# GpSimd takes the softmax divisions and six copies of means in the lead; the last token tile is finished in halves

## Chip, cores and metric
One Trainium2 chip; the kernel runs on one of its cores. The metric is the device time of one execution in microseconds (us). Engines: TensorE (PE, its weight loads PEld), VectorE (DVE), ScalarE (ACT), GpSimd (POOL), SyncE (SP, which issues the DMAs).

## What is computed
Local attention for 2 batches, 8 heads, 768 positions and heads of 64, then two feed-forward layers over the 1536 tokens (model width 512, hidden width 2048), all in float32:

```python
k_sum = k.reshape(B, H, nb, 32, D).max(axis=3)
v_sum = v.reshape(B, H, nb, 32, D).mean(axis=3)
scores_l = scale * q @ k.T where |i - j| < 16 else -1e9
scores_s = scale * q @ k_sum.T + log(32)
a = softmax(concat([scores_l, scores_s]))
x = a @ concat([v, v_sum])                    # (1536, 512)
x = maximum(x @ w_in, 0) ** 2 @ w_out         # first layer
h = x @ w_in2;  out = (h * sigmoid(h)) @ w_out2
```

## The kernel before
Attention works on 24 tiles of 64 queries (12 a batch). A tile's 8 heads lie as 4 pairs; each query sees 96 window keys and 24 block keys, 120 columns (NK). For a tile g: scores `pss` (TensorE, 16 products), minus the scores with the mask and the row minimum (VectorE, `minimum`, line 414, from PSUM with the mask in SBUF), exponentials with their sums z (ScalarE, line 419), a guard and the reciprocal r (VectorE, lines 439 and 442), the division T*r (`norm`, lines 445 to 450), transposes `psa` (TensorE, line 456), their copy a (ScalarE), products `av` with the values (TensorE), and then x split into a high part (ScalarE) and a low part (VectorE).

The layers use three float32r products for one exact one: high by high, high by low, low by high. Every weight arrives as raw 64-bit numbers and is decoded: a scale `c` on ScalarE, a shift (line 306), a sign (310) and a join (314) on VectorE, then a high part on ScalarE and a low part on VectorE (262). Blocks of 512 tokens go through 16 chunks of the hidden width: h (`gemm1`), relu and square, split, `gemm2` into four accumulators.

The **lead** is tiles 0 to 7 (NLEAD), the 512 tokens of the first block. Until all eight have their x, no h can run. Their value tiles are one tile `vlead`: 96 rows by DMA, 24 rows with the block means, the same for all tiles of the batch. The means come out of six products `psv`, and ScalarE copies them from PSUM into eight tiles (`vmean`, two instructions of four tiles each).

The order of the whole first part (the lead, the first layer's first two blocks, the other 16 attention tiles) on every engine and on SP's queue is written by `first_order`: a list scheduler with a cost and a due time for each step, the due times moved by a table `shift`; the kernel then issues the steps in that order. Later blocks are plain loops. `layer2_block` is the second layer: chunk by chunk, with `rows` giving each token tile of 128 its products; the last two chunks (LAG) are taken tile by tile, each tile is then copied out of PSUM, VectorE and ScalarE in turn, and stored by SP.

## Time and profile before

| | us |
|---|---|
| runs | 610.33 median of 3 (609.83 to 612.03) |
| profiled execution | 611.61 |
| its span | 609.6 |
| TensorE busy | 595.1 |
| VectorE busy | 326.4 |
| ScalarE busy | 323.4 |
| GpSimd busy | 9.6 |

The span is from the first to the last instruction that the profiler saw; the execution's own time has 2.0 us more around it. Busy times are sums over the whole span, so they hide that stretches differ. TensorE's mean granted clock was 0.997 of full.

### The profile page before, as it was taken

Reading aid. Unit: us, or ns where it says so; the run is one execution under the profiler, and the core shown is the slowest. Engines: PE = TensorE matmul, PEld = TensorE weight load, DVE = VectorE, ACT = ScalarE, POOL = GpSimd, SP = SyncE. Lnnn points to the kernel's source line nnn. Section 1 sums busy time; section 2 is a strip of 40 time slices with the busy share of each in tenths; the row PEclk is TensorE's granted clock in tenths of the full one; section 3 lists DMA queues with packets and bytes.
Section 4 is the critical chain, followed back from the end, with each engine's and each line's share of the span. In section 5 each row is a group of like instructions: output and inputs, shape, how many; then the busy total and the mean of one; then the engine's idle time right before and its main releaser. Section 6 shows DMA issues by size and latency. Waiting matters only on the chain.

```text
span 609.6 us, 8844 instructions
## 1 busy us (share of the span) xinstructions
PE 595.1 (98%) x3242; PEld 483.3 (79%) x3242; DVE 326.4 (54%) x779; ACT 323.4 (53%) x727; POOL 9.6 (2%) x25
## 2 busy tenths in 40 slices
PE   6999999899999999999999999999999999999997
PEld 5578788668987878888888888888888888888886
DVE  4999999994433332385556686764322222322222
ACT  4999987788766764565555554443321222212221
POOL 0000000110000000000000000000000000000000
PEclk8999999999999999999999999999999999999999
DMA  8987888676545642365662345425400223400211
GB/s 301 300 281 271 291 294 271 229 253 223 182 170 164 215 152 94 115 203 184 199 202 74 105 138 184 161 104 187 158 0 2 91 84 103 138 1 5 99 35 69
DMA packets 36618, 96.50 MB, mean 158 GB/s; under 512 B 3936, under 2 KB 11232, under 8 KB 36576
## 3 DMA queue, kind: packets, MB, share of 16 engines
q1 hardware_dynamic: 36576, 95.95, 47.8%
q8 instruction: 25, 0.41, 0.3%
q14 instruction: 17, 0.14, 0.1%
HBM read 74.96 MB, written 20.97 MB: 157 GB/s over the span
## 4 chain that ended last, share of the span: by engine, by line
PE 78%; DVE 6%; DMA 3%; ACT 1%; issue 0%; SPq 0%; ACTq 0%
PE acc L254 38%; PE h L254 37%; DMA t_kv<-in_vT_dram 2%; PE pss L254 2%; PE av L254 1%; PE psa L456 1%; DMA raw_wi<-in_w_in_dram 1%; DMA kw<-in_kW_dram 1%; DVE raw_wi L310 1%; DVE c_wo L314 1%; DVE c_wi L314 1%; DVE vsumT L637 1%; DVE g L262 0%; DVE raw_wo L310 0%; DVE wi L262 0%; DVE wo L262 0%
## 5 line engine op out<-in xcount | busy, mean ns | idle before, releaser
L254 PE MATMUL h<-xt,wi 128*128 128x512 f32 (+1 forms) x600 | 141.9, 385 | 0.5 <-DVE xt L262 0.4
L254 PE MATMUL acc<-g,wo 128*128 128x512 f32 (+1 forms) x600 | 141.5, 384 | 0.0
L254 PE MATMUL h<-xt,wj 128*128 128x512 f32 x576 | 139.0, 390 | 0.0
L254 PEld LDWEIGHTS h<-xt,wj 128*128 128x128 f32 x576 | 108.1, 188 | 23.6 <-DVE r L262 0.2
L254 PEld LDWEIGHTS h<-xt,wi 128*128 128x128 f32 x600 | 108.3, 188 | 22.9 <-DVE xt L262 0.7
L254 PEld LDWEIGHTS acc<-g,wo 128*128 128x128 f32 x600 | 108.2, 188 | 22.3 <-issue 1.0
L262 DVE TENSOR_TENSOR g<-r,g 128x512 fp32r<-128x512 f32 (+1 forms) x98 | 67.1, 685 | 70.5 <-ACT g L258 69.9
L262 DVE TENSOR_TENSOR r<-h,r 128x512 f32<-128x512 f32 x48 | 33.2, 692 | 114.3 <-ACT r L510 113.7
L510 ACT ACTIVATE r<-h 128x512 f32<-128x512 f32 x48 | 28.7, 598 | 117.4 <-PE h L254 117.4
L258 ACT ACTIVATE g<-r 128x512 fp32r<-128x512 f32 (+1 forms) x98 | 61.0, 623 | 35.8 <-DVE r L262 34.5
L254 PE MATMUL acc<-wq,g 128*128 128x512 f32 x240 | 57.3, 389 | 0.0
L254 PE MATMUL acc<-wo,g 128*128 128x512 f32 x216 | 53.6, 397 | 0.0
L254 PEld LDWEIGHTS acc<-wq,g 128*128 128x128 f32 x240 | 45.1, 188 | 9.3
L254 PEld LDWEIGHTS acc<-wo,g 128*128 128x128 f32 x216 | 40.6, 188 | 9.7
L419 ACT ACTIVATE T<-T,m 128x120 f32<-128x120 f32 x96 | 36.6, 384 | 6.1 <-DVE m L414 6.1
L693 ACT ACTIVATE r<-h 128x512 f32<-128x512 f32 (+1 forms) x34 | 19.1, 561 | 24.3 <-PE h L254 24.3
L254 PE MATMUL acc<-wp,g 128*128 128x512 f32 x120 | 28.8, 389 | 0.0
L506 ACT ACTIVATE r<-h 128x512 f32<-128x512 f32 x16 | 9.6, 597 | 36.0 <-PE h L254 36.0
L254 PEld LDWEIGHTS acc<-wp,g 128*128 128x128 f32 x120 | 22.5, 188 | 4.7
L414 DVE CUSTOM_DVE_ANT_0 T<-pss,cst_sb 128x120 f32<-128x120 f32 x96 | 21.8, 274 | 5.3 <-PE pss L254 5.1
L262 DVE TENSOR_TENSOR wj<-c_wj,wj 128x512 fp32r<-128x512 f32 x16 | 11.1, 692 | 22.6 <-ACT wj L258 22.6
L448 ACT ACTIVATE T<-T,r 128x120 f32<-128x120 f32 x64 | 20.0, 383 | 2.4 <-DVE r L442 2.4
(78 smaller groups left out, 540.8 us busy)
## 6 DMA issues: line engine op xcount, KB each, us to landing
raw_wo<-in_w_out_dram SPq DMA_DIRECT2D x22, 512.0 KB, 4.4
wq<-split SPq DMA_DIRECT2D x20, 512.0 KB, 3.3
raw_wi<-in_w_in_dram SPq DMA_DIRECT2D x16, 512.0 KB, 5.0
split<-wo SPq DMA_DIRECT2D x16, 512.0 KB, 3.1
raw_wj<-in_w_in_dram SPq DMA_DIRECT2D x16, 512.0 KB, 4.0
wo<-split SPq DMA_DIRECT2D x16, 512.0 KB, 3.3
raw_wp<-in_w_out_dram SPq DMA_DIRECT2D x10, 512.0 KB, 3.6
split<-wp SPq DMA_DIRECT2D x10, 512.0 KB, 2.8
```

The lines of the kernel that those rows point to most:

```text
L254: pe.matmul(o, l, r, **kw)
L258: return act.activation(out=o, in_=i, func=AF.Copy, scale=scale)
L262: return eng.tensor_tensor(out=o, in0=a, in1=b, op=op)
L310: vec.scalar_tensor_tensor(out=low, in0=high, scalar=SIGN, in1=low, op0=ALU.bitwise_and, op1=ALU.bitwise_or)
L314: vec.scalar_tensor_tensor(out=c, in0=c, scalar=3, in1=raws.pop(name)[:, :, 0], op0=ALU.logical_shift_left, op1=ALU.bitwise_or)
L414: vec.tensor_tensor_reduce(out=d["T"][:, c], in0=d["ps"][:, c], in1=cst_sb[:, kind * NK:kind * NK + NK], scale=-0.125, scalar=3.0e38, op0= ...
L419: act.activation(out=d["T"][:, c], in_=d["T"][:, c], func=AF.Exp, bias=d["m"][:, c:c + 1], scale=-1.0, accum_out=d["z"][:, c:c + 1])
L448: act.activation(out=T[:, c], in_=T[:, c], func=AF.Copy, scale=r[:, c:c + 1])
L456: pe.transpose(ps[0:NK, c], d["T"][:, c], id_sb)
L506: act.activation(out=r, in_=h, func=AF.Relu)
L510: act.activation(out=r, in_=h, func=AF.Sigmoid)
L693: act.activation(out=rs[n][:, cc], in_=hs.pop(n)[:, cc], func=AF.Relu)
```

## The change
GpSimd takes two things over in the lead. It divides the exponentials by their sums for tiles 0 to 7 (VectorE did), and ScalarE copies the means from PSUM to tiles 0 and 1 alone; GpSimd copies them on from there, within SBUF, to tiles 2 and 3 and then to tiles 4 to 7. The planner's table, some due times and the distance of loads are changed, so the order of the whole first part is another one. In the second layer the very last token tile's last two chunks, copy and store are done in two halves of 256 columns.

```diff
+MEANS = [(2, 4), (4, 8)]
...
-    shift = dict(psl=-3,ttl=3,exl=-6,ze=-4,nt=2,psa=-6,a=-0.5,vs=1,vmean=1,av=0.5,xh=-2,xl=-2,ksl=0.5,kwl=3,ksum=-6)
+    shift = dict(psl=-2,ttl=2,nt=0.5,psa=-6,a=2,vs=3,ksl=2,kwl=-1,ksum=1)
...
-        return 0.25 * g if g < NLEAD else 50 + 14 * (g - NLEAD) if g < TPB else 120 + 4 * (g - TPB) if g < 2 * NLEAD else 155 + 10 * (g - 2 * NLEAD)
+        return 0.25 * g if g < NLEAD else 50 + 20 * (g - NLEAD) if g < TPB else 120 + 4 * (g - TPB) if g < 2 * NLEAD else 160 + 11 * (g - 2 * NLEAD)
...
-    for i in range(NLEAD // NGRP):
-        op("act", "vmean", i, 1.9, -5, [("vs", c, M) for c in range(6)] + [("vl", i, 0)] * 0)
+    op("act", "vmean", 0, 1.05, -5, [("vs", c, M) for c in range(6)])
+    for i, (g0, g1) in enumerate(MEANS):
+        op("pool", "vmore", i, .3 + .5 * (g1 - g0), -5 + i, [("vmean", 0, A)])
...
-            op("vec", "nt", g, .78, due, [("rc", g, .1)])
+            op("pool", "nt", g, 1.4, due, [("rc", g, A)])
...
-        load("raw", (x, s), 524, chunk_due(s) - 14 + .5 * (x == "wo") - 100 * (not i),
+        load("raw", (x, s), 524, chunk_due(s) - 18 + .5 * (x == "wo") - 100 * (not i),
...
-                load("c2", s, 262, due - 20, [("scr", s, 0), ("st2", chunks[i - NRAW], A) if s < NRAW else ("lo2", s - NRAW, A)])
+                load("c2", s, 262, due - 14, [("scr", s, 0), ("st2", chunks[i - NRAW], A) if s < NRAW else ("lo2", s - NRAW, A)])
...
-                vec.tensor_scalar(out=T[:, c], in0=T[:, c], scalar1=r[:, c:c + 1], scalar2=None, op0=ALU.mult)
+                eng.tensor_scalar(out=T[:, c], in0=T[:, c], scalar1=r[:, c:c + 1], scalar2=None, op0=ALU.mult)
...
+        def spread(eng, g0, g1, means):
+            copy(eng, vlead[NWIN:NK, g0:g1].rearrange("p g h d -> p g (h d)"),
+                 bass.AP(means.tensor, means.offset, [means.ap[0], [0, g1 - g0], [1, DM]]))
+
+        def vmean(_):
+            spread(act, 0, MEANS[0][0], psv[NWIN:NK])
+
+        def vmore(i):
+            spread(pool, *MEANS[i], vlead[NWIN:NK, 0])
...
+        parts = [(k, slice(0, DM)) for k in range(n // P)]
+        if tok0 + n == NTOK:
+            k = n // P - 1
+            parts[-1:] = [(k, slice(0, 256)), (k, slice(256, DM))]
         with tc.manual_schedule(engines={pe.engine}):
-            for k in range(n // P):
-                rows(acc[k], k, range(NF - LAG, NF), gs, wos)
-        for k in range(n // P):
-            o = raw_p.tile([P, 512], F32, tag="raw", name=f"ro{tok0}_{k}")
-            copy(act if k % 2 else vec, o, acc[k])
-            sp.dma_start(out=out[tok0 + k * P:tok0 + (k + 1) * P, :], in_=o)
+            for k, cols in parts:
+                rows(acc[k], k, range(NF - LAG, NF), gs, wos, cols)
+        for i, (k, cols) in enumerate(parts):
+            o = raw_p.tile([P, 512], F32, tag="raw", name=f"ro{tok0}_{i}")
+            copy(act if i % 2 else vec, o[:, cols], acc[k][:, cols])
+            sp.dma_start(out=out[tok0 + k * P:tok0 + (k + 1) * P, cols], in_=o[:, cols])
```

The order on GpSimd, from its last memset of the lead on (T is a tile's exponentials, r the reciprocals, qd a copy of queries for the later tiles 12 and up). Before:

```order
L569 MEMSET t_ksum0_2_178 128x16
L370 MEMSET share_108 32x1 x4
L569 MEMSET t_ksum0_3_180 128x16
L259 COPY qd0_101<-qr0_99 128x256
L259 COPY qd1_102<-qr1_100 128x256
```

Now, from the instruction behind that memset on (the ISA row sets GpSimd up for what follows):

```order
L452 ISA
L452 TENSOR_SCALAR T0_134<-T0_134,r0_138 128x120 x4
L452 TENSOR_SCALAR T1_139<-T1_139,r1_143 128x120 x4
L452 TENSOR_SCALAR T2_144<-T2_144,r2_148 128x120 x4
L452 TENSOR_SCALAR T3_149<-T3_149,r3_153 128x120 x4
L452 TENSOR_SCALAR T4_154<-T4_154,r4_158 128x120 x4
L452 TENSOR_SCALAR T5_159<-T5_159,r5_163 128x120 x4
L452 TENSOR_SCALAR T6_164<-T6_164,r6_168 128x120 x4
L452 TENSOR_SCALAR T7_169<-T7_169,r7_173 128x120 x4
L261 COPY vlead_105<-vlead_105 24x1024
L261 COPY vlead_105<-vlead_105 24x2048
L261 COPY qd0_101<-qr0_99 128x256
```

Eight tiles of four divisions and the two copies of means stand in front of the first copy of queries.

The order on ScalarE and VectorE before the first h. ScalarE first, from the exponentials of tile 6 before, and of tile 7 now (a is the copy of a tile's transposes, xt0 the high part of x, c and w the weights). Before:

```order
L419 ACTIVATE T6_164,z6_167<-T6_164,m6_166 128x120 x4
L419 ACTIVATE T7_169,z7_172<-T7_169,m7_171 128x120 x4
L258 ACTIVATE c_wi0_452<-raw_wi0_201 128x512
L258 ACTIVATE a3_150<-psa3_406 120x512
L258 ACTIVATE a4_155<-psa4_424 120x512
L258 ACTIVATE wi0_469<-c_wi0_452 128x512
L258 ACTIVATE vlead_105<-psv0_118 24x2048 x2
L258 ACTIVATE xt0_85<-av0_485 128x4x64
L258 ACTIVATE xt0_85<-av1_495 128x4x64
L258 ACTIVATE xt0_85<-av2_506 128x4x64
L258 ACTIVATE a5_160<-psa5_462 120x512
L258 ACTIVATE xt0_85<-av3_516 128x4x64
```

Now:

```order
L421 ACTIVATE T7_169,z7_172<-T7_169,m7_171 128x120 x4
L260 ACTIVATE a0_135<-psa0_349 120x512
L260 ACTIVATE a1_140<-psa1_371 120x512
L260 ACTIVATE c_wi0_447<-raw_wi0_201 128x512
L260 ACTIVATE vlead_105<-psv0_118 24x1024
L260 ACTIVATE a2_145<-psa2_442 120x512
L260 ACTIVATE wi0_473<-c_wi0_447 128x512
L260 ACTIVATE xt0_85<-av0_463 128x4x64
L260 ACTIVATE a3_150<-psa3_452 120x512
L260 ACTIVATE a4_155<-psa4_475 120x512
L260 ACTIVATE xt0_85<-av1_482 128x4x64
L260 ACTIVATE c_wo0_512<-raw_wo0_205 128x512
```

The copies of a of tiles 0 to 2, which stood among the exponentials, stand behind them, and the copies of means went from two of 24x2048 to one of 24x1024. VectorE's, from the first join of weights before and from the first shift now, before:

```order
L314 SCALAR_TENSOR_TENSOR c_wi0_452<-c_wi0_452,raw_wi0_201 128x512
L442 RECIPROCAL r7_173<-z7_172 128x4
L306 TENSOR_SCALAR raw_wo0_205<-raw_wo0_205 128x512
L450 TENSOR_SCALAR T7_169<-T7_169,r7_173 128x120 x4
L262 TENSOR_TENSOR wi0_469<-c_wi0_452,wi0_469 128x512
L310 SCALAR_TENSOR_TENSOR raw_wo0_205<-raw_wo0_205 128x512
L306 TENSOR_SCALAR raw_wi1_207<-raw_wi1_207 128x512
L310 SCALAR_TENSOR_TENSOR raw_wi1_207<-raw_wi1_207 128x512
L306 TENSOR_SCALAR raw_wo1_215<-raw_wo1_215 128x512
L310 SCALAR_TENSOR_TENSOR raw_wo1_215<-raw_wo1_215 128x512
L262 TENSOR_TENSOR xt0_85<-av0_485,xt0_85 128x4x64
L262 TENSOR_TENSOR xt0_85<-av1_495,xt0_85 128x4x64
```

Now:

```order
L308 TENSOR_SCALAR raw_wi0_201<-raw_wi0_201 128x512
L312 SCALAR_TENSOR_TENSOR raw_wi0_201<-raw_wi0_201 128x512
L316 SCALAR_TENSOR_TENSOR c_wi0_447<-c_wi0_447,raw_wi0_201 128x512
L308 TENSOR_SCALAR raw_wo0_205<-raw_wo0_205 128x512
L312 SCALAR_TENSOR_TENSOR raw_wo0_205<-raw_wo0_205 128x512
L264 TENSOR_TENSOR wi0_473<-c_wi0_447,wi0_473 128x512
L264 TENSOR_TENSOR xt0_85<-av0_463,xt0_85 128x4x64
L308 TENSOR_SCALAR raw_wi1_207<-raw_wi1_207 128x512
L312 SCALAR_TENSOR_TENSOR raw_wi1_207<-raw_wi1_207 128x512
L264 TENSOR_TENSOR xt0_85<-av1_482,xt0_85 128x4x64
L308 TENSOR_SCALAR raw_wo1_215<-raw_wo1_215 128x512
L264 TENSOR_TENSOR xt0_85<-av2_495,xt0_85 128x4x64
```

The divisions are gone, and the low parts of x stand one by one between the steps of the weights.

The order on TensorE around the first h (pss8 and pss9 are the scores of tiles 8 and 9, acc0 the first layer's accumulators). Before:

```order
L254 MATMUL av6_562<-a6_165,vlead_105 64x64 x8
L254 MATMUL av7_576<-a7_170,vlead_105 64x64 x8
L254 MATMUL pss9_587<-kw9_233,qr1_100 64x120 x8
L254 MATMUL h0_0_615<-xt0_85,wi0_469 128x512 x12
L254 MATMUL h0_1_645<-xt0_85,wi1_628 128x512 x12
L254 MATMUL pss8_680<-kw8_225,qr0_99 64x120 x8
L254 MATMUL acc0_0_694<-g0_0_666,wo0_603 128x512 x3
```

Now:

```order
L256 MATMUL av6_570<-a6_165,vlead_105 64x64 x8
L256 MATMUL av7_583<-a7_170,vlead_105 64x64 x8
L256 MATMUL h0_0_607<-xt0_85,wi0_473 128x512 x12
L256 MATMUL h0_1_637<-xt0_85,wi1_604 128x512 x12
L256 MATMUL pss8_667<-kw8_225,qr0_99 64x120 x8
L256 MATMUL acc0_0_681<-g0_0_658,wo0_543 128x512 x3
```

Tile 9's scores no longer stand ahead of h; they come after six more h and g products of the first layer.

## Rows read from the trace of the kernel before

**Rows 1.** The page, first part: busy us, share and instructions of each engine.
```profile
PE 595.1 (98%) x3242; PEld 483.3 (79%) x3242; DVE 326.4 (54%) x779; ACT 323.4 (53%) x727; POOL 9.6 (2%) x25
```

**Rows 2.** By stretch: length, busy of PE, PEld, DVE, ACT, POOL; clock, DMA, GB/s.
```profile
12.00:13.00 1.00, 1.00 (x12) 1.00 (x14) 0.97 (x3) 1.00 (x4) 0.00 (x0) 0.50 1.06 389
...
30.00:36.00 6.00, 4.59 (x128) 4.21 (x130) 5.64 (x16) 5.98 (x12) 0.00 (x0) 1.00 1.01 264
...
40.00:60.00 20.00, 20.00 (x102) 16.39 (x101) 19.72 (x53) 19.69 (x48) 0.00 (x0) 1.00 0.89 309
...
140.00:160.00 20.00, 20.00 (x161) 17.59 (x161) 10.00 (x29) 15.88 (x43) 0.66 (x1) 1.00 0.61 202
```

**Rows 3.** TensorE's timeline, 36 to 134: start, us, instructions, idle before and releaser.
```profile
38.45 5.51 PE L254 MATMUL h<-xt,wi 128*128 128x512 f32 x23 [0.38 <-DVE xt L262]
43.88 1.22 PE L254 MATMUL pss<-kw,qr 64*64 64x120 f32 x16
...
110.89 0.28 PE L643 MATMUL psv<-cst_sb,vsumT 128*24 128x128 f32 x1 [0.35 <-DVE vsumT L637]
...
115.41 1.04 PE L254 MATMUL pss<-kw,qd 64*64 64x120 f32 x16 [1.50 <-DMA raw_wi<-in_w_in_dram]
...
123.70 1.18 PE L456 MATMUL psa<-cst_sb,T 128*120 128x128 f32 x4 [0.36 <-ACT T L448]
...
133.31 1.04 PE L254 MATMUL pss<-kw,qd 64*64 64x120 f32 x16 [0.68 <-DMA kw<-in_kW_dram]
```

**Rows 4.** ScalarE's timeline in the lead.
```profile
18.97 0.38 ACT L419 ACTIVATE T<-T,m 128x120 f32<-128x120 f32 x1
...
26.45 0.68 ACT L258 ACTIVATE c_wi<-raw_wi 128x512 f32<-128x512 f32 x1
...
27.01 1.08 ACT L258 ACTIVATE a<-psa 120x512 f32<-120x512 f32 x2
...
28.94 3.64 ACT L258 ACTIVATE vlead<-psv 24x2048 f32<-24x2048 f32 x2
...
32.60 0.94 ACT L258 ACTIVATE xt<-av 128x256 fp32r<-128x256 f32 x3
```

**Rows 5.** VectorE's timeline in the lead.
```profile
16.40 0.85 DVE L450 TENSOR_SCALAR T<-T,r 128x120 f32<-128x120 f32 x4
...
26.31 0.42 DVE L306 TENSOR_SCALAR raw_wi<-raw_wi 128x512 int32<-128x512 int32 x1
...
26.76 0.69 DVE L310 SCALAR_TENSOR_TENSOR raw_wi<-raw_wi 128x512 int32<-128x512 int32 x1
...
33.02 1.09 DVE L262 TENSOR_TENSOR xt<-av,xt 128x256 fp32r<-128x256 f32 x3 [0.26 <-ACT xt L258]
...
37.97 0.42 DVE L262 TENSOR_TENSOR xt<-av,xt 128x256 fp32r<-128x256 f32 x1
```

**Rows 6.** First load of weights, and landing times of raw_wi issued before 30 us.
```profile
9.52 1.69 SPq L290 DMA_DIRECT2D raw_wi<-in_w_in_dram  x1
...
DMA to landing us min/median/max: 16.1/16.2/16.5
```

**Rows 7.** GpSimd's timeline.
```profile
0.74 0.14 POOL L368 MEMSET share<- 128x44 f32 x1 [0.29 <-POOLq L895]
...
1.48 0.12 POOL L569 MEMSET t_ksum<- 128x16 f32 x1
81.25 0.63 POOL L259 COPY qd<-qr 128x256 f32<-128x256 f32 x1 [79.66 <-DMA qr<-in_qW_dram]
```

**Rows 8.** VectorE's timeline beside that copy.
```profile
81.31 1.13 DVE L310 SCALAR_TENSOR_TENSOR raw_wi<-raw_wi 128x512 int32<-128x512 int32 x1
```

**Rows 9.** 36 products of 256 columns; ScalarE's last copy; the last four stores (KB, us).
```profile
155.58 4.48 PE L254 MATMUL acc<-g,wo 128*128 128x256 f32 x36
...
605.98 0.60 ACT L258 ACTIVATE ro<-acc 128x512 f32<-128x512 f32 x1 [2.12 <-PE acc L254]
...
out_dram<-ro SPq DMA_DIRECT2D x4, 256.0 KB, 2.0
```

More of the change, by code (lines that the diff above doesn't have):

```diff
@@ L125, in first_order @@
         if g < NLEAD:
-            op("vec", "nt", g, .78, due, [("rc", g, .1)])
+            op("pool", "nt", g, 1.4, due, [("rc", g, A)])
         else:
             op("act", "nt", g, 1.2, due, [("rc", g, A)])
-        op("pe", "psa", g, .62, due - 2, [("nt", g, -.1)], bank=("att", "a", g))
+        op("pe", "psa", g, .62, due - 2, [("nt", g, A)], bank=("att", "a", g))
         op("act", "a", g, .56, due, [("psa", g, M)] + [("av", g - 1, M)] * (g > NLEAD))
-        values = [("vl", g // NGRP, 0), ("vmean", g // NGRP, A)] if g < NLEAD else [("vf", g, 0), ("vfm", g % NVF, A)]
+        values = [("vl", g // NGRP, 0), ("vmean", 0, A) if g < MEANS[0][0] else ("vmore", int(g >= MEANS[1][0]), A)] if g < NLEAD else [("vf", g, 0), ("vfm", g % NVF, A)]
         op("pe", "av", g, .66, due, values + [("a", g, A)] + [("vfc", g, A)] * (TPB <= g < TPB + NVF),
@@ L617, in vs @@
             mm(psv[NWIN:NK], share[:, lo:lo + NSUM], vrows[c // 2][:, c % 2], start=(c == 0), stop=(c == S // P - 1))
-        def vmean(i):
-            means = psv[NWIN:NK]
-            copy(act, vlead[NWIN:NK, i * NGRP:i * NGRP + NGRP].rearrange("p g h d -> p g (h d)"),
-                 bass.AP(means.tensor, means.offset, [means.ap[0], [0, NGRP], means.ap[1]]))
+        def spread(eng, g0, g1, means):
[5 more added lines that the diff above has]
+            spread(pool, *MEANS[i], vlead[NWIN:NK, 0])
         def vfm(i):
@@ L743, in xh @@
             x_high(g)
-        do = dict(kt=kt, q=q, cst=cst_, vr=vr, vl=vl, ksum=ksum_, kwl=kwl, ksl=ksl, vs=vs, vmean=vmean, vfm=vfm, kv=kv, kvr=kvr,
+        do = dict(kt=kt, q=q, cst=cst_, vr=vr, vl=vl, ksum=ksum_, kwl=kwl, ksl=ksl, vs=vs, vmean=vmean, vmore=vmore, vfm=vfm, kv=kv, kvr=kvr,
                   vend=vend, vendc=vendc, vfc=vfc, kw=kw_load, qr=q_load, vf=v_load, kwc=k_sums,
                   pss=scores, ttr=minima, exp=exps, ze=guard, rc=inverse, psl=psl, ttl=lambda a: minimum(*a),
-                  exl=lambda a: exponential(*a), nt=lambda g: norm(g, vec if g < NLEAD else act),
+                  exl=lambda a: exponential(*a), nt=lambda g: norm(g, pool if g < NLEAD else act),
                   psa=transposes, a=a_copy, av=products, xh=xh, xl=x_low, raw=raw, sc=sc,
@@ L774, in layer1_block, with rows @@
         finish1(x, acc)
-    def rows(acc, k, js, gs, wos):
+    def rows(acc, k, js, gs, wos, cols=slice(0, DM)):
         ts_ = slice(k * P, (k + 1) * P)
+        how = dict(skip_group_check=True)
         for j in js:
             g, w = gs[j], wos[j]
-            mm(acc, g[:, 0, ts_], w[:, 0], start=(j == 0), stop=False)
-            mm(acc, g[:, 0, ts_], w[:, 1], start=False, stop=False)
-            mm(acc, g[:, 1, ts_], w[:, 0], start=False, stop=(j == NF - 1))
+            mm(acc[:, cols], g[:, 0, ts_], w[:, 0, cols], start=(j == 0), stop=False, **how)
+            mm(acc[:, cols], g[:, 0, ts_], w[:, 1, cols], start=False, stop=False, **how)
+            mm(acc[:, cols], g[:, 1, ts_], w[:, 0, cols], start=False, stop=(j == NF - 1), **how)
     def layer2_block(load, tok0, n):
```

## The prediction, made before the changed kernel was run

> **What bounds the kernel now.** I read the page's busy shares first: TensorE is busy 98% of the span [rows 1], so only three places are left to gain in: the lead before the steady products, the stalls among them, and the tail. The table by stretch says who sets each. In 30 to 36 us ScalarE is busy 5.98 of 6.00 us and VectorE 5.64, while TensorE has 4.59; in 40 to 60 us all three are full; from 140 on TensorE alone is [rows 2]. TensorE's timeline gives the places. The first products h run from 38.45 us, after 0.38 us of waiting for the last low part of x on VectorE. After that, TensorE waits four times: 0.35, 1.50, 0.36 and 0.68 us, together 2.89 us, all between 110 and 134 us [rows 3]. From there to the end it never waits. So the end moves by: when h's second product can start (I call it S, now 38.45), plus products moved behind S, plus what changes in those 2.89 us, plus the tail.
>
> **ScalarE in the lead.** Before, ScalarE's chain sets S: the exponentials of tile 4 start at 18.97 at 0.38 us each, three copies of a stand among them, and the two copies of means of 24x2048 take 3.64 us [rows 4]. In the change the 16 exponentials of tiles 4 to 7 stand together: 18.97 + 16 x 0.38 = 25.0 us. Behind them stand 23 instructions up to the last high part of x: 8 copies of a at 0.54 (two took 1.08), one copy of means of 24x1024 (a quarter of 3.64, 0.91), 6 copies of weights at 0.56 (26.45 to 27.01), 8 high parts at 0.31 (three took 0.94) [rows 4]: 4.3 + 0.9 + 3.4 + 2.5 = 11.1, so 36.1 us. The weight copies wo0 and c_wo1 are new ahead of it (1.1 us); they stood behind it before and are not lost.
>
> **VectorE in the lead.** It loses 8 x 0.85 = 6.8 us of divisions [rows 5], but most of that was time in which ScalarE set the pace. What counts starts when the first weights are there: issued at 9.52, landed 16.1 us later, 25.6 us [rows 6]. From there the change has 23 instructions to the last low part: 5 shifts at 0.42, 8 joins and signs and 2 weight low parts at 0.69, 8 low parts of x at 0.42, less 0.085 where one starts ahead of the other's end (three of 0.42 took 1.09) [rows 5]: 2.1 + 6.9 + 3.4 - 1.9 = 10.5 us. With 0.5 us of its own waits (for c_wi0 and wi0 on ScalarE) it ends at 36.6. If nothing else came in, S would be 36.6.
>
> **New waits.** Tile 0's transposes on TensorE now wait for GpSimd instead of VectorE, until 16.4 + 1.1 (worked out below) = 17.5, and tile 1's after them; behind them stand half of tile 6's scores and tile 7's. The exponentials of tile 6 want theirs at 18.97 + 8 x 0.38 = 22.0, so over 4 us cover that. VectorE's small guards of the sums may be held up by a division each, 8 x 0.15 us; the 6.8 us that VectorE lost there cover them.
>
> **GpSimd comes in.** While GpSimd copied 128x256 in 0.63 us from 81.25 [rows 7], VectorE's join of two SBUF operands, begun at 81.31, took 1.13 us in place of 0.69 [rows 5, 8]: 0.44 us more. So a GpSimd instruction holds such VectorE instructions for its time less 0.19 us. Of the 23 instructions 15 are of that kind (shifts, joins, weight low parts); the 8 low parts of x have one operand in PSUM, and I take them as free.
>
> What GpSimd's new work takes no row shows. Bounds: a line through its memsets (128x16 0.12, 128x44 0.14) is 0.7 ns an element, one through memset and copy (0.12, 0.63 for 256) is 2.1 [rows 7]. A division of 128x120 is then 0.19 to 0.34 us; I take the middle, 0.27, as it also reads a scalar. The copies of means read and write consecutive elements, as the memsets write them and unlike the copy, which gathers every fourth; I take a value a quarter of the way up, 1.05 ns: 1.18 us for 24x1024, 2.25 for 24x2048 (bounds 0.83 to 2.2 and 1.5 to 4.4). The divisions keep up with ScalarE (4 x 0.27 = 1.1 us a tile against 1.5 of exponentials), so after 25.6 only tile 7's four remain: 4 x 0.08 us of hold; the copies hold 0.99 + 2.06. Together 3.35 us; VectorE's waits vanish in it, and one low part of x (0.35) passes beside the long copy. S = 25.6 + 10.5 + 3.35 - 0.35 = 39.1, 0.65 later than before. ScalarE's 36.1 is then no bound. The copies begin when ScalarE has the first means, 25.0 + 1.1 + 0.6 + 0.9 = 27.6, and end by about 32 with a join or two between; tile 4's products are wanted at about 33 in ScalarE's order, so that wait costs nothing.
>
> The Trainium skill (SBUF — State Buffer, section SBUF: two separate sides) speaks against the change: whichever of the two engines begins first keeps the shared port pair for the whole instruction. Counted so, the holds would be 4 x 0.27 + 1.18 + 2.25 = 4.5 us, and the sum below 1.15 higher. The trace agrees that one blocks the other, but with 0.44 of 0.63 us [rows 7, 8].
>
> The Trainium skill (GPSIMD Engine Reference, section 3.1) puts a short one-input body at 1.03 cycles an element at 1.2 GHz: an estimate of 0.88 and 1.76 us for the two copies of means. By that the sum would be 0.8 lower. No row here shows such a copy.
>
> Ahead of the divisions stands a GpSimd set-up instruction without a wait, at about 1.6 us; the first division is wanted at 16.4 (VectorE's first division stands at 16.40 [rows 5]). Its price is not in the trace; 14.8 us cover it, so I take nothing.
>
> **TensorE's order.** Tile 9's scores stood before h and were hidden; now they stand behind S: +1.2 us (16 products took 1.22 [rows 3]).
>
> **The stalls at 110 to 134 us.** The long one, 1.50, is tile 12's scores waiting for a late VectorE (its copy of key sums). From the last low part of x to that copy VectorE had, by the order, 38 weight and g low parts of 128x512 and 4 of x; now 35 and 3, and two small copies more: 3 x 0.60 + 0.34 - 2 x 0.12 = 1.9 us less, while TensorE has the same products ahead but one tile's scores more and one tile's av fewer, 0.5 us more. Slack grows by 2.4: the 1.50 and the 0.35 (whose slack grows more) go. Of the other two, which hang on tile 12's and 14's softmax, I count half: 1.85 + 0.55 = 2.4 of 2.89 gone. Bounds: none to all. On SP the loads of tile 10 and of batch 1's keys change places with weights; SP stands waiting for VectorE to free a raw buffer in either order, so I take nothing, but the row names a load of raw_wi as what ended the 1.50 [rows 3]: if loads set it, it stays, which is rival (b).
>
> **The tail.** The last six products of 512 columns become 12 of 256: at 4.48/36 = 0.124 [rows 9] that is 1.49 in place of 1.36, +0.13. The last copy is 128x256 instead of 128x512, 0.42 [rows 5] for 0.60 [rows 9], -0.18; its store has half the bytes of one that lands in 2.0 us [rows 9], between 0 and -1.0; I take -0.25, nearer to none. In all -0.3, bounds 0 to -1.0.
>
> **The sum**, on the profiled execution (611.61 us, of which the span is 609.6): +0.65 + 1.2 - 2.4 - 0.3 = -0.85, so 610.8. The profiled execution stands 1.28 above the median of the runs, 610.33, and I carry the difference over: 609.5 us.
>
> **Rivals.**
> (a) GpSimd costs nothing: its instructions fall where VectorE waits anyway, or a copy of 24 partitions holds nothing up. Then S = 36.6, -1.85 in place of +0.65: sum -3.35, 607.0 us. For it: VectorE waits for ScalarE in this stretch; against: 15 of its 23 instructions can be held up, 7.7 of the 10.5 us.
> (b) VectorE is not late any less at 110 us: its lateness came from waits on loads, which stay. All 2.89 us remain: 609.5 + 2.4 = 611.9.
> (c) Slower: GpSimd copies at its copy's line. Divisions of 0.34 run late (16.4 + 8 x 1.36 = 27.3), 5 of them after 25.6 hold 0.75, the means 2.07 + 4.2: 7.0 us, S = 42.75. Sum +4.3 + 1.2 - 2.4 - 0.3 = +2.8: 613.1. TensorE would then have stood nearly idle for some 6 us before h; in 12 to 13 us it was granted 0.50, the lower level, 1.2 GHz, with TensorE full [rows 2]. If h's first 3 us ran so, +1.5: 614.6. The place is the copy of 24x2048; it decides slower against faster when the holds pass 3.35 + 0.85 = 4.2 us.
> (d) The tail's halves buy nothing: +0.3, inside the forecast's own range.
>
> **Numbers.** Half a percent, 3.05 us, is about what a measurement can tell from no change: 607.28 to 613.38. Forecast 0.44, (a) 0.24, (b) 0.17, (c) 0.15. Faster takes most of (a) and the low edge of the forecast: 0.22. Slower takes the half of (c) with the clock and a little of its rest: 0.10. Same 0.68. The range 606.6 to 612.9 leaves out the lower third of (a) and the upper two thirds of (c).
>
> **What would show it.** Right: h's second product near 39 us in TensorE's timeline, VectorE's joins at 26 to 33 us longer than 0.69, GpSimd's copies near 1.2 and 2.3 us, no wait over 1 us at 110 to 120. Wrong: h at 37 with joins at 0.69 (a); the 1.5 us wait still there (b); a GpSimd copy over 4 us, or a granted clock under 1.00 at h (c).

## The result and the profile after

The changed kernel takes 618.54 us (median of 4 runs, 617.07 to 620.10) against 610.55 for the kernel before beside it: ratio 1.0128, 95% interval 1.0096 to 1.0160. It is slower by 8.0 us; the forecast was 609.5, its range ended at 612.9. The profiled execution has a span of 618.3 us; S, the start of h's second product, is 45.79 us in place of 38.45 [rows 3]. S and all rows of a kernel come from its one profiled execution, which need not be a typical one: here it is the longest of the four, and the four go with their mean granted clock (617.07 us at 0.994, the others 618.07 to 620.10 at 0.989).

The page's first part and the table by stretch (columns as in [rows 2]):

```profile
PE 601.7 (97%) x3248; PEld 486.2 (79%) x3248; DVE 322.3 (52%) x748; ACT 320.9 (52%) x726; POOL 33.1 (5%) x59
```

```profile
16.00:25.00 9.00, 7.45 (x61) 4.48 (x59) 5.21 (x45) 8.42 (x45) 9.00 (x17) 0.84 1.05 274
25.00:30.00 5.00, 5.00 (x8) 1.02 (x7) 3.11 (x7) 1.50 (x3) 5.00 (x7) 0.61 1.04 379
30.00:36.00 6.00, 4.52 (x48) 2.56 (x46) 2.17 (x5) 4.22 (x8) 6.00 (x10) 1.00 0.92 248
36.00:40.00 4.00, 2.32 (x34) 1.96 (x36) 1.91 (x6) 1.40 (x3) 3.40 (x3) 0.89 0.02 7
40.00:46.00 6.00, 4.76 (x82) 3.86 (x79) 4.86 (x12) 4.89 (x12) 0.00 (x0) 0.79 0.37 131
```

One stretch of the kernel before, beside [rows 2]:

```profile
25.00:30.00 5.00, 4.13 (x16) 1.41 (x14) 4.83 (x21) 4.78 (x14) 0.00 (x0) 1.00 1.04 394
```

GpSimd is full from 16 to 39 us. VectorE and ScalarE, nearly full before, now stand idle more than half of 25 to 40 us, and TensorE's granted clock was below full in four of the five stretches, lowest from 25 to 30 us with 0.61. GpSimd's timeline, and its groups by shape in the lead (busy us, mean ns of one):

```profile
15.99 20.46 POOL L452 TENSOR_SCALAR T<-T,r 128x120 f32<-128x120 f32 x32 [14.42 <-DVE m L416]
36.52 2.94 POOL L261 COPY vlead<-vlead 24x1024 f32<-24x1024 f32 x2
```

```profile
L452 POOL TENSOR_SCALAR T<-T,r 128x120 f32<-128x120 f32 x32 | 20.5, 660 | 14.4 <-DVE m L416 14.4
L261 POOL COPY vlead<-vlead 24x2048 f32<-24x2048 f32 x1 | 1.9, 1893 | 0.0
L261 POOL COPY vlead<-vlead 24x1024 f32<-24x1024 f32 x1 | 1.1, 1107 | 0.1
```

A division takes 0.66 us on average where the prediction had 0.27; the two copies of means take 1.11 and 1.89 where it had 1.18 and 2.25. Since 32 divisions stand in front of the copies, those end at 39.46. TensorE's timeline:

```profile
22.00 0.68 PE L256 MATMUL pss<-kws,qrlead 64*64 64x120 f32 x4 [0.39 <-DVE m L416]
23.06 0.68 PE L256 MATMUL pss<-kws,qrlead 64*64 64x120 f32 x4 [0.39 <-DVE m L416]
23.67 7.90 PE L256 MATMUL psv<-vrows,share 128*24 128x512 f32 x12
...
37.68 0.69 PE L256 MATMUL av<-a,vlead 120*64 120x64 f32 x16 [3.05 <-POOL vlead L261]
...
45.08 0.49 PE L256 MATMUL h<-xt,wi 128*128 128x512 f32 x1 [1.02 <-ACT xt L260]
45.79 5.51 PE L256 MATMUL h<-xt,wi 128*128 128x512 f32 x23 [0.22 <-DVE xt L264]
```

Before, the products of means (psv) ran from 21.39 to 28.10, with transposes between them:

```profile
21.39 1.04 PE L254 MATMUL psv<-vrows,share 128*24 128x512 f32 x2
...
24.49 3.61 PE L254 MATMUL psv<-vrows,share 128*24 128x512 f32 x8
```

In both kernels they stand behind the scores of tile 7. Now the last two of its four pairs of scores (four products each) wait 0.39 us each for VectorE; the products of means start 2.28 us later, at 23.67, and take 7.90 us. Tile 2's products then wait 3.05 us for GpSimd's means. ScalarE and VectorE stand behind the same products:

```profile
31.61 1.02 ACT L260 ACTIVATE vlead<-psv 24x1024 f32<-24x1024 f32 x1 [5.11 <-PE psv L256]
```

```profile
33.80 0.73 DVE L264 TENSOR_TENSOR wi<-c_wi,wi 128x512 fp32r<-128x512 f32 x1 [5.48 <-ACT wi L260]
```

ScalarE waits 5.11 us for the means and has them copied at 32.63 (31.61 + 1.02); GpSimd, still dividing, copies them on only from 36.52. VectorE waits 5.48 us for a weight's high part that stands behind the means on ScalarE. Behind S little changed: the last product ended at 605.94 before, 567.5 us after S, and now at 614.79 (606.40 + 8.39), 569.0 after S. Of the waits [rows 3] names, one of 1.33 us is left at 128.88; others of 0.25 to 0.27 stand at 104.59, 108.78, 133.11 and 141.72, 2.4 us in all against 2.89.

The last two copies, on ScalarE and VectorE:

```profile
614.83 0.38 ACT L260 ACTIVATE ro<-acc 128x256 f32<-128x256 f32 x1 [2.19 <-PE acc L256]
615.24 0.42 DVE L261 COPY ro<-acc 128x256 f32<-128x256 f32 x1 [1.15 <-ACT ro L260]
```

The first half's copy starts at 614.83, when the products of both halves have ended (614.79), and the second half's when the first has ended.

### The profile page after: what moved, and what is told of

It is laid out like the page before. It is cut to its first block, busy times and chain, and to the rows that moved or that the text cites. A ratio compares the mean times of both kernels' runs of the same rounds, so it can differ in the third digit from the quotient of the medians.

```text
span 618.3 us, 8876 instructions
## 1 busy us (share of the span) xinstructions
PE 601.7 (97%) x3248; PEld 486.2 (79%) x3248; DVE 322.3 (52%) x748; ACT 320.9 (52%) x726; POOL 33.1 (5%) x59
## 4 chain that ended last, share of the span: by engine, by line
PE 79%; DVE 7%; ACT 3%; DMA 2%; issue 1%; ACTq 0%; DVEq 0%
PE acc L256 38%; PE h L256 37%; PE pss L256 2%; PE av L256 1%; DMA t_kv<-in_vT_dram 1%; PE psa L458 1%; DVE wi L264 1%; DVE c_wo L316 1%; DVE c_wi L316 1%; DVE g L264 1%; DVE raw_wo L312 1%; DMA t_kv<-in_kT_dram 1%; DMA kw<-in_kW_dram 1%; DVE wo L264 0%; DVE raw_wi L312 0%
## 5 line engine op out<-in xcount | busy, mean ns | idle before, releaser
L264 DVE TENSOR_TENSOR r<-h,r 128x512 f32<-128x512 f32 x48 | 33.2, 692 | 114.2 <-ACT r L512 113.7
L256 PE MATMUL acc<-wq,g 128*128 128x512 f32 (+1 forms) x246 | 57.4, 384 | 0.0
L452 POOL TENSOR_SCALAR T<-T,r 128x120 f32<-128x120 f32 x32 | 20.5, 660 | 14.4 <-DVE m L416 14.4
```

What stands on the lines that cost most here:

```text
L256: pe.matmul(o, l, r, **kw)
L264: return eng.tensor_tensor(out=o, in0=a, in1=b, op=op)
L452: eng.tensor_scalar(out=T[:, c], in0=T[:, c], scalar1=r[:, c:c + 1], scalar2=None, op0=ALU.mult)
```

## Experiments

Below, a ratio is to the kernel before, with its 95% interval, and S is from the profiled execution; where TensorE ran into h without a wait, the start of h is given. S also moves with the first loads: TensorE's first scores start at 6.94 us in the kernel before, where they wait 1.46 us for the queries' load, and between 5.65 and 6.97 in the other runs. A difference of less than about 1 us in S therefore says little by itself. Diffs are shortened, and leave out what only repeats.

### The parts, one at a time, in the order of before

**Divisions alone.** Order of every other engine as before.
```diff
-                vec.tensor_scalar(out=T[:, c], in0=T[:, c], scalar1=r[:, c:c + 1], ...
+                eng.tensor_scalar(out=T[:, c], in0=T[:, c], scalar1=r[:, c:c + 1], ...
-        nt=lambda g: norm(g, vec if g < NLEAD else act)
+        nt=lambda g: norm(g, pool if g < NLEAD else act)
```


> The kernel before, with the lead's 32 divisions on GpSimd and nothing else; every other engine's order as before. Theory 1 (the divisions' length, 0.56 us each and longer beside VectorE's decode, costs by itself): GpSimd runs from 16.4 to about 36 us, the last tiles' transposes wait for it, S (the start of h's second product) 41 to 43 us in place of 38.45, time 613.5 to 616. Theory 2 (only the new order loses, GpSimd's divisions fit where they are asked for): S 38 to 39, 609.5 to 611.

Measured: 1.0093 (1.0066 to 1.0119), 615.4 us, S 40.85. TensorE's timeline, tile 6's transposes, one by one behind a division each:

```profile
30.73 0.33 PE L456 MATMUL psa<-cst_sb,T 128*120 128x128 f32 x1 [0.16 <-POOL T L450]
31.75 0.33 PE L456 MATMUL psa<-cst_sb,T 128*120 128x128 f32 x1 [0.70 <-POOL T L450]
32.81 0.33 PE L456 MATMUL psa<-cst_sb,T 128*120 128x128 f32 x1 [0.74 <-POOL T L450]
33.63 0.33 PE L456 MATMUL psa<-cst_sb,T 128*120 128x128 f32 x1 [0.49 <-POOL T L450]
```

The divisions cost by themselves, as theory 1 has it; S came out 0.15 below its bound, with first scores that started 1.2 us earlier than in the kernel before.

**Copies of means alone.** ScalarE copies to tiles 0 and 1, GpSimd on to 2 to 7.
```diff
-            copy(act, vlead[..., i * 4:i * 4 + 4], means)
+            (i == 0) copy(act, vlead[..., 0:2], means)
+            (i == 1) copy(pool, vlead[..., 2:4], vlead[..., 0]); copy(pool, vlead[..., 4:8], vlead[..., 0])
```


> The kernel before, with the copies of means to lead tiles 2 to 7 on GpSimd (24x1024 and 24x2048 out of tile 0) and nothing else; ScalarE copies to tiles 0 and 1 alone. Theory (these copies are 1.1 and 1.9 us and begin as soon as ScalarE's first copy has ended, with no division in front of them): ScalarE, which sets S, has 2.7 us less to do; VectorE's shifts or joins beside the copies lose up to 1.4 us; S 36.8 to 38.2, 608.5 to 610.5. Rival (GpSimd's copies cost VectorE as much as ScalarE gains, and VectorE is then the bound): S 38.5 to 40, 610.5 to 612.

Measured: 1.0075 (1.0060 to 1.0089), 615.4 us, h from 41.53; worse than either expected. GpSimd, VectorE and TensorE in their timelines, and the table by stretch:

```profile
29.75 4.06 POOL L259 COPY vlead<-vlead 24x1024 f32<-24x1024 f32 x2 [28.17 <-ACT vlead L258]
```

```profile
30.65 1.41 DVE L310 SCALAR_TENSOR_TENSOR raw_wi<-raw_wi 128x512 int32<-128x512 int32 x1
31.98 2.12 DVE L306 TENSOR_SCALAR raw_wo<-raw_wo 128x512 int32<-128x512 int32 x1
...
34.74 1.08 DVE L262 TENSOR_TENSOR xt<-av,xt 128x256 fp32r<-128x256 f32 x3
```

```profile
35.26 1.12 PE L254 MATMUL av<-a,vlead 120*64 120x64 f32 x16 [2.55 <-issue]
...
37.35 2.83 PE L254 MATMUL av<-a,vlead 120*64 120x64 f32 x48
```

```profile
30.00:36.00 6.00, 2.71 (x74) 2.46 (x72) 5.93 (x9) 2.41 (x6) 3.81 (x2) 0.85 0.91 247
36.00:40.00 4.00, 4.00 (x60) 3.54 (x56) 2.67 (x8) 2.46 (x6) 0.00 (x0) 0.50 0.04 15
```

GpSimd's copies run from 29.75 to 33.81. The sign that starts beside the first takes 1.41 us (0.69 alone [rows 5]), the shift that starts beside the second 2.12 (0.42): 2.4 us lost. So VectorE's first low part of x starts at 34.74 in place of 33.02 [rows 5], and tile 4's products, which go into the PSUM tile that it frees, start behind it, after 2.55 us of idle time. TensorE, busy 2.71 of 6 us, is then granted 0.50, the lower level (1.2 GHz), from 36 to 40 us: the same 48 products of tiles 5 to 7 take 2.83 us, before 1.64:

```profile
34.70 1.64 PE L254 MATMUL av<-a,vlead 120*64 120x64 f32 x48
```

**Tail alone** (the diff's last two hunks).

> The kernel before, with the last token tile's two last chunks, copy and store in halves and nothing else. In the changed kernel's trace the first half's copy began only when the last product of both halves had ended, and the second half's copy when the first half's had ended. So: from TensorE's last product to the end of the span 3.5 us in place of 3.66, products 0.1 longer, time within 0.3 us of the kernel before. Rival (the prediction's sum): 0.3 to 1.0 us faster.

Measured: 0.9996 (0.9983 to 1.0009). From the last product to the end it is 3.5 us, as expected, and the time shows no difference; the rival falls.

**The table alone**: no GpSimd work in the lead, all orders planned anew with the changed shifts and due times.
```diff
-            op("pool", "nt", g, 1.4, due, [("rc", g, A)])
+            op("vec", "nt", g, .78, due, [("rc", g, .1)])
-            spread(pool, *MEANS[i], vlead[NWIN:NK, 0])
+            spread(act, *MEANS[i], psv[NWIN:NK])
```


> The changed kernel without any GpSimd work in the lead: divisions on VectorE, all copies of means on ScalarE, the planner told so and the order planned anew with the changed table of shifts and due times; the tail in halves stays. Theory (the loss is GpSimd's: its long queue of divisions and its copies of means that hold VectorE): S 38.5 to 40 us, TensorE's clock 1.00 at h, 610.5 to 613. Rival (the changed table loses by itself, with or without GpSimd): 614 or more.

Measured: 1.0029 (1.0017 to 1.0041), 612.6 us, h from 38.56. So divisions, means and table cost 5.7, 4.6 and 1.8 us of some 611 one at a time; the change, with all three, costs 7.8 by its ratio, less than their sum of 12.1. That their waits overlap is the likely reason; it is not shown. The order of this run is not the changed kernel's either, since it was planned anew: the changed kernel's own order without any GpSimd work was not run.

### What the copies of means cost by

**In six pieces**, otherwise as the means alone.
```diff
-  copy(pool, vlead[..., 2:4], ...); copy(pool, vlead[..., 4:8], ...)
+  for g in range(2, 8): copy(pool, vlead[..., g], vlead[..., 0])
```


> The kernel before with the copies of means to tiles 2 to 7 on GpSimd, as in the run that did this alone (615.4 us), but in six copies of 24x512 in place of 24x1024 and 24x2048. Theory (a GpSimd copy holds a VectorE shift or join that comes after it until that copy has ended): each copy is 0.55 to 0.75 us, so no shift or join on VectorE is over 1.2 us, where one took 2.12; VectorE is 0.8 to 1.6 us earlier, S (the start of h's second product) 39.5 to 40.8 in place of 41.7, 612 to 614. Rival (it is the sum of GpSimd's time that counts, however it is cut): S 41.5 to 42.5, 615 to 616.5.

Measured: 1.0009 (0.9998 to 1.0020), 612.2 us, S 39.14, a little better than the theory's edge. VectorE, the sign and the two shifts beside the copies:

```profile
30.88 0.98 DVE L310 SCALAR_TENSOR_TENSOR raw_wi<-raw_wi 128x512 int32<-128x512 int32 x1
31.79 0.84 DVE L306 TENSOR_SCALAR raw_wo<-raw_wo 128x512 int32<-128x512 int32 x1
...
34.55 0.41 DVE L306 TENSOR_SCALAR raw_wi<-raw_wi 128x512 int32<-128x512 int32 x1
```

No instruction is over 1.0 us. GpSimd's time did not fall (5.46 us for six against 4.06 for two), so its sum is not what counts, and the rival falls. Three things improved together: VectorE lost 1.3 us to the copies in place of 2.4, TensorE got the means tile by tile (its longest wait was 0.99 us), and its granted clock stayed 1.00 from 36 to 40 us. The run does not separate them.

**Products nobody reads in the wait**, with the two long copies as in the means alone.
```diff
+            if g == 4:
+                for _ in range(10): mm(idle_out, w0[:, 0, 0:P], w0[:, 0], start=True, stop=True)
             products(g)
```


> The kernel of the means on GpSimd alone (615.4 us), with ten products of 512 columns more on TensorE, whose result nobody reads, in front of tile 4's products, where TensorE waited 2.55 us and its granted clock then was 0.50 from 36 to 40 us. Theory (the clock is a third or so of the loss): the granted clock stays over 0.9 from 36 to 40 us, tile 5 to 7's products and tile 9's scores take 2.9 us in place of 4.3, S 39.8 to 40.6, 612.5 to 614. Rival (the late VectorE alone sets S, the low clock is hidden beside it): S 41.3 or more, 615 to 616.

Measured: 1.0030 (1.0018 to 1.0042), 613.5 us, S 40.00. TensorE's timeline and the table by stretch:

```profile
32.43 2.56 PE L254 MATMUL idle_out<-wi 128*128 128x512 f32 x10
...
36.26 1.62 PE L254 MATMUL av<-a,vlead 120*64 120x64 f32 x48
...
40.00 5.51 PE L254 MATMUL h<-xt,wi 128*128 128x512 f32 x23 [0.37 <-DVE xt L262]
```

```profile
36.00:40.00 4.00, 3.53 (x69) 2.79 (x67) 3.94 (x11) 3.77 (x9) 0.00 (x0) 1.00 0.15 55
```

The granted clock stays 1.00, and the 48 products take 1.62 us. By the ratios the clock was 2.7 us of the 4.6, give or take 1.2. The other 1.8 are left with the long copies, which still hold VectorE here.

**By a DMA** from tile 0, ahead of two loads of keys and one of weights on SP.
```diff
+  sp.dma_start(out=vlead[..., 2:8], in_=vlead[..., 0] repeated six times)
```


> The kernel before with the copies of means to tiles 2 to 7 made by one DMA from tile 0, issued by SP behind the loads for tile 9 and ahead of two loads of keys; GpSimd does nothing in the lead, ScalarE copies to tiles 0 and 1 alone. Theory (GpSimd's copies cost by what they hold on VectorE, not by taking work off ScalarE): VectorE's shifts stay at 0.42, ScalarE is 2.7 us earlier, the DMA lands by 32.5, S 36.5 to 38, 608.5 to 610.5. Rival (the means come late through any detour, and TensorE's wait for them is what costs): TensorE waits over 1.5 us for tile 2's products, S 38.5 or more, 611 or more.

Measured: 1.0109 (1.0089 to 1.0130), 617.9 us, S 46.49. The rival, and more than it: issued at 30.74, the means are there at 38.6, as TensorE's timeline shows:

```profile
38.62 2.83 PE L263 MATMUL av<-a,vlead 120*64 120x64 f32 x48 [7.50 <-DMA vlead<-vlead]
```

### What a division costs by

**Odd tiles only**, in the order of before (`pool if g % 2 else vec`).

> The kernel before, with the divisions of lead tiles 1, 3, 5 and 7 on GpSimd and nothing else. Theory (GpSimd's divisions cost when their sum, 32 x 0.56 us, is longer than ScalarE's exponentials beside it; 16 of them are not): GpSimd's last division ends by 30 us, S 37.8 to 38.8, 609.5 to 611. Rival (each division on GpSimd delays its tile's transposes, and the scores behind them): S over 39.5, 612 or more.

Measured: 1.0016 (1.0001 to 1.0031), 612.25 us, S 38.84. S at the theory's edge, the time in the rival's range. GpSimd's last division ended at 33.2, not by 30: tile 7's four took 4.40 us beside VectorE's decode, where four alone take 2.3. No gain from the 3.4 us that VectorE no longer spends on divisions.

**One instruction a tile**, all tiles, in the order of before.
```diff
-  four of: eng.tensor_scalar(out=T[:, c], in0=T[:, c], scalar1=r[:, c:c + 1], ...)
+  eng.tensor_tensor(out=T, in0=T, in1=r repeated 120 times a pair, op=ALU.mult)
```


> The kernel before with the lead's divisions on GpSimd alone, each tile's four instructions of 120 columns as one of 480 with the reciprocals spread by a zero stride. If most of the 0.56 us is per instruction: under 1.3 us a tile, GpSimd ends by 29 us, S 38 to 39, 609.5 to 611.5. If most is per element: 1.8 to 2.3 us a tile, S 40 to 41.5, 613 to 616.

Measured: 1.0008 (0.9992 to 1.0023), 612.1 us, S 37.71. GpSimd's group here, that of the changed kernel's first 16 divisions, and TensorE's timeline:

```profile
L450 POOL TENSOR_TENSOR T<-T,r 128x480 f32<-128x480 f32 x8 | 7.9, 991 | 19.3 <-ACT T L419 14.0 <-DVE r L442 5.3
```

```profile
L452 POOL TENSOR_SCALAR T<-T,r 128x120 f32<-128x120 f32 x16 | 9.0, 581 | 14.4 <-DVE m L416 14.4
```

```profile
111.18 0.28 PE L643 MATMUL psv<-cst_sb,vsumT 128*24 128x128 f32 x1 [1.38 <-DVE vsumT L637]
```

480 columns take 0.99 us, 120 took 0.58 alone: an estimate from the two is 0.44 us per instruction and 1.1 ns a column, though the forms differ. So the loss of the divisions is gone: the time, 0.6 us over the first case's range, can't be told from that of the kernel before. S is 0.74 us earlier than before, but no gain of the move: the first scores started 0.87 us earlier in this execution (6.07 against 6.94), as its first loads landed earlier. What became of those 0.74 us is of use: the wait at 111 us, 0.35 before [rows 3], is 1.38, so an earlier S comes back as a wait for VectorE, which is full from 40 to 60 us [rows 2].

### Parts of the change undone

**Divisions back on VectorE**, the rest of the order kept (`pool` to `vec` in `nt`).

> The changed kernel with the divisions of the lead back on VectorE, every engine's order of the rest as in the changed kernel; GpSimd keeps the copies of means. Theory (GpSimd's 32 divisions of 0.56 us each, one behind the other until 36.5 us, set the lead): S, the start of h's second product, goes from 45.8 back to 38 to 39.5 us, TensorE's granted clock stays 1.00 from 20 to 36 us, time 610 to 612. Rival 1 (the new written order loses, wherever the divisions are): S stays over 43 us, 616 to 618. Rival 2 (GpSimd's copies of means hold VectorE, as the prediction had it): joins at 26 to 33 us longer than 0.9 us, S over 41, 613 to 615.

Measured: 1.0116 (1.0102 to 1.0131), 619.2 us: no gain, against the theory; rival 1 by S, and beyond its time. S is 43.50, and TensorE's first 23 products of h take 7.12 us, not 5.51. TensorE's timeline, and VectorE's shift beside GpSimd's second copy:

```profile
24.76 0.68 PE L256 MATMUL pss<-kws,qrlead 64*64 64x120 f32 x4 [0.41 <-DVE m L416]
25.37 6.29 PE L256 MATMUL psv<-vrows,share 128*24 128x512 f32 x12
...
43.50 7.12 PE L256 MATMUL h<-xt,wi 128*128 128x512 f32 x23 [0.53 <-DVE xt L264]
```

```profile
34.93 1.79 DVE L308 TENSOR_SCALAR raw_wi<-raw_wi 128x512 int32<-128x512 int32 x1
```

The products of means start still later, at 25.37, behind scores that wait for VectorE pair by pair; a shift is held 1.79 us. So the divisions on GpSimd are not the only cause: the written order, made for a VectorE without divisions, makes the means late by itself. How much of this run's loss is the order and how much GpSimd's copies, it does not say.

**Means on ScalarE**, the rest kept.

> The changed kernel with the six other copies of means on ScalarE, from PSUM, in the place in its order where GpSimd's stood in the plan; the divisions stay on GpSimd. Theory (the length of the divisions alone): the last division still ends at 35 to 36.5 us, S 43 to 46, 616 to 619, as ScalarE gets 2.7 us more to do behind the first means. Rival (what costs is that the copies of means stand behind the divisions in GpSimd's queue, and the products of tiles 2 to 7 behind them): S 39 to 41.5, 611 to 614.

Measured: 1.0060 (1.0042 to 1.0078), 616.1 us, S 42.98. The theory's time at its lower edge. In the profile the clock stayed 1.00 to 30 us and the products of means took 5.33 us:

```profile
23.70 5.33 PE L256 MATMUL psv<-vrows,share 128*24 128x512 f32 x12
```

That is 2.57 of the 2.81 us by which S is earlier than in the changed kernel, and it is not shown to come from the edit: the two kernels differ only behind these products, which start at 23.70 and 23.67, and yet from 22 to 25 us one was granted 1.00 and the other, the changed kernel, 0.51:

```profile
22.00:25.00 3.00, 2.22 (x11) 0.96 (x12) 1.82 (x14) 2.70 (x15) 3.00 (x7) 1.00 1.01 304
```

```profile
22.00:25.00 3.00, 2.61 (x10) 0.94 (x11) 1.54 (x12) 2.42 (x13) 3.00 (x7) 0.51 1.00 362
```

The six runs, 613.46 to 617.84 us, go with their mean granted clock, 0.996 to 0.989.

**Half of the divisions back** (odd tiles on GpSimd).

> The changed kernel with the divisions of the even lead tiles on VectorE, of the odd ones on GpSimd, all orders else as in the changed kernel. Theory: 16 divisions of 0.56 us on GpSimd are 9.0 us within the 12 us of exponentials, so GpSimd keeps up: the last ends by 27 us, the copies of means by 33, S 37 to 39, 608.5 to 611. Rival (any division on GpSimd holds VectorE's decode or TensorE's transposes up): S over 41 us, 613 or more.

Measured: 1.0102 (1.0084 to 1.0119), 618.2 us, S 41.78. GpSimd's last division ended at 31.8, not 27, and the time did not move: the rival's time, but with the products of means starting as late as in the change (23.98, ending at 29.31).

**The true cost for the planner** (2.4 in place of 1.4 us a tile).

> The changed kernel with the planner told that a tile's four divisions take GpSimd 2.4 us, where it had 1.4; the divisions stay on GpSimd, the whole order is planned anew. Theory (the length of the divisions): the order can't mend it, S 42 to 45 us, 614.5 to 618. Rival (the order was merely planned for a wrong cost): S under 40.5 us, 610 to 612.5.

Measured: 1.0194 (1.0178 to 1.0209), 623.9 us, worse than both theories; tile 2's products wait 6.49 us for the means behind the divisions.

**Scores of tiles 6 and 7 ahead of their minima**, in the changed kernel.
```diff
+    for g in (6, 7): the four ttl steps of g go behind the step psl (g, 3)
```


> The changed kernel with one thing moved in the written order: the minima of lead tiles 6 and 7 stand behind all four pairs of scores of their tile, so that TensorE need not wait for VectorE between two pairs; GpSimd's work as in the changed kernel. Theory 2 (TensorE reaches the products of the means late, since its scores wait pair by pair, and ScalarE and VectorE stand idle for 5 us behind the first means): the products of means begin at about 21.5 in place of 23.7 us, ScalarE's wait for them falls from 5.1 to under 3 us, S 43 to 44.5, 616 to 617.5, as GpSimd's copies of means, which end at 39.5, are the next bound. Theory 1 (GpSimd's divisions alone set S): S stays at 45.5 or more, 618 to 619.

Measured: 1.0137 (1.0121 to 1.0154), 619.1 us, S 44.67. S as theory 2, the time as theory 1: the products of means now run from 21.33, ScalarE waits 1.56 us for them, and TensorE 6.59 us for GpSimd (its timeline):

```profile
21.33 5.33 PE L262 MATMUL psv<-vrows,share 128*24 128x512 f32 x12
...
36.30 1.12 PE L262 MATMUL av<-a,vlead 120*64 120x64 f32 x16 [6.59 <-POOL vlead L267]
```

**The same, with odd tiles alone on GpSimd.**

> The same written order as the run before it (scores of tiles 6 and 7 ahead of their minima), and the divisions of the even lead tiles on VectorE, of the odd ones on GpSimd. If the late products of means and the long GpSimd queue are the two causes, and there is no third: S 38.5 to 40 us, TensorE's clock 1.00 at h, 610.5 to 612.5. If something else in the written order costs: S over 41, 613 or more.

Measured: 1.0054 (1.0033 to 1.0076), 614.4 us, S 40.25: over half of the loss is gone (1.28% to 0.54%), the time 1.9 us over the expected range. Either step alone gained little or nothing (1.0137 for the order, 1.0102 for the odd tiles): where one cause stays, taking the other away is worth little.

**The same, with the means on ScalarE too.**

> The kernel with odd tiles' divisions on GpSimd and scores ahead of minima (614.4 us), with the copies of means to tiles 2 to 7 on ScalarE as well, so that GpSimd copies nothing in the lead. Theory (beside that kernel's VectorE, GpSimd's copies of means cost the shift and join they hold, some 2 us, and TensorE's wait of 1.66 us for the means): no shift over 0.5 us on VectorE, S 38.5 to 40.3 (ScalarE has 2.7 us more to do), 612 to 614. Rival (those copies cost nothing, the order does): S 41 or more, 614.5 or more.

Measured: 1.0077 (1.0058 to 1.0096), 616.0 us, S 40.32: S at the theory's edge, the time as the rival; the 2.7 us of copies came back on ScalarE, where tile 5's transposes then wait 2.92 us.

### The change mended

**In its own order**: one division of 128x480 a tile, six copies of means.

> The changed kernel, its written order kept, with each lead tile's division as one GpSimd instruction of 128x480 and the means to tiles 2 to 7 as six copies of 24x512. Theory (long division queue and long holds cost most; what is left is the order: products of means behind the scores, tile 9's scores behind h): GpSimd's last division ends by 27.5 us, the copies by 35.5, S 39.5 to 41.3, TensorE's clock 1.00 from 36 to 40 us, 612 to 614.5 in place of 618.5. Rival (another cause in the changed kernel is not found yet): 615.5 or more.

Measured: 1.0079 (1.0062 to 1.0096), 616.5 us, S 43.75 (in a profiled execution of 619.58 us). Worse than the theory, better than the change by 0.5%. The products of means are late again (TensorE's timeline):

```profile
24.92 7.90 PE L256 MATMUL psv<-vrows,share 128*24 128x512 f32 x12
```

7.90 us at a granted clock of 0.50 (25 to 30 us), with VectorE idle 3.60 us behind it. The late start is the order's; the low clock, 2.6 us of the delay, came in this execution as in that of the changed kernel, and not in two others of the same order (5.33 us). So what is left is in part the order, and the rest stays open. Both mends together with the scores ahead of their minima were not run.

**In the order of before**, both moves.

> The kernel before, its order kept, with both moves in the mended form (one GpSimd division of 128x480 a tile, six copies of 24x512 on GpSimd). Theory 1 (ScalarE and VectorE both get time in the lead, but VectorE is full from 40 to 110 us and the long wait there takes a gain in S back): S 37.3 to 38.8, TensorE's waits between 105 and 120 us together 2.2 us or more, 610 to 612.5, no measurable gain. Theory 2 (a gain in S reaches the end): S as above and 608 to 609.8.

Measured: 1.0037 (1.0025 to 1.0049), 614.1 us, h from 39.28: outside both. VectorE met GpSimd more often (a shift of 0.98 us beside a division, shifts of 0.83 and 0.84 beside copies, 0.42 alone [rows 5]); TensorE waited 2.01 us for the means and was granted 0.65 from 36 to 40 us. No version tried beats the kernel before.

## Why the prediction was wrong

- **GpSimd's division** (0.27, bounds 0.19 to 0.34): 0.58 alone, 0.66 on average. This failed first. The bounds were drawn through memsets and a gathering copy; none of these rows reads a scalar per partition, and the price turned out to be mostly per instruction. "Only tile 7's four remain after 25.6" became 15, and GpSimd's copies, which it can make from 32.63 on, began at 36.52.
- **ScalarE in the lead** ("the first means at 27.6"): they were there at 32.63. The prediction's own sum for ScalarE held: the exponentials ended at 25.0. But TensorE's products of means, started 2.28 us late behind tile 7's scores and slowed by 2.57 us of low clock, ended at 31.57, and ScalarE idled 5.11 us. With VectorE's minima moved behind the scores they start at 21.33, so the order of scores and minima is what made them start late. The prediction added up ScalarE's and VectorE's orders; of TensorE's it timed tile 0's transposes and took 4 us of slack for the rest, and the products of means it did not time.
- **GpSimd holding VectorE** (holds of 0.99 and 2.06 us for the copies): measured 0.72 and 1.70 in the means alone, right in kind and nearly in size. In the changed kernel it did not decide: VectorE was idle, and GpSimd was the one held (four divisions of 0.83 to 1.08 us beside the decode from 25 us on). The copies' own lengths (1.11 and 1.89 for 1.18 and 2.25) came near by a guess, "a quarter of the way up". The Trainium skill (SBUF — State Buffer, section SBUF: two separate sides) says that whichever begins first keeps the port pair for its whole instruction. The traces agree: a shift begun at 31.98 ended 0.29 us behind the copy's end, and six short copies hold less than two long ones. The prediction had set that rule aside for 0.44 of 0.63 us; of the 0.19 us between, 0.06 is that the join began later than the copy, and 0.13 shows in the shift as well (0.29 of its 0.42 us lay behind the copy).
- **Rival (c)** named the right side and mechanism in part: S 42.75 and a lower clock. The clock fell elsewhere in the changed kernel: 0.61 from 25 to 30 us made the products of means 2.6 us longer than the 5.33 of the run with means on ScalarE, while h's first 23 products took the full clock's 5.51. With 0.15 it was given too little.
- **TensorE's order** (+1.2 for tile 9): the end moved 1.5 us more than S. Tile 9's 1.2 and the tail's 0.1, less 0.5 of waits, make 0.8 of it; the rest no row here explains.
- **The stalls** (-2.4): at most 0.5 came. The slack was to come from a VectorE with less to do. VectorE is as good as full behind S in either kernel (13.70 of 14 us from 46 to 60 now), and the run with one division a tile shows an earlier S turned into a longer wait. That the loads set it, as rival (b) has it, is not excluded.
- **The tail** (-0.3): 0, rival (d). The first half's copy waits for all products. The Trainium skill (PSUM — Partial Sum Buffer, section Terms) says two engines must not be in one bank at once; the program orders them so here, and the trace shows the two copies one behind the other.

Open: how much of the change's loss is the order and how much GpSimd, since each alters the waits of the other and the clock changes with them; and why the clock falls in one execution and not in another. Executions of one kernel in the changed order differ by 2 to 4 us, the longer mostly with the lower mean granted clock, as in the run with means on ScalarE.

## What to carry to other kernels

Before moving small elementwise work to GpSimd, time one instruction of that shape there: here four of 120 columns cost 2.2 us and one of 480 cost 1.0, the difference between 5.7 us lost and none measurable. Give a helper engine short instructions where another shares its path to SBUF, and look where its queue puts a late, long item behind early ones. In a hand-planned order a moved step changes the waits of every queue: add up each engine's chain, TensorE's too, and what its clock does while it waits.

## What the hardware showed unexpectedly

A GpSimd division of 128x120 with a scalar per partition takes 0.58 us, and 0.79 to 1.12 beside VectorE's decode; VectorE, in turn, was held 1.70 us by one copy. Ten useless products in a wait of 2.55 us were worth 2.7 us by the ratios; the granted clock behind them stayed 1.00 instead of 0.50. A DMA within SBUF of 288 KB took 7.9 us from issue to use, with the DMA engines 0.91 busy from 30 to 36 us.
